# Attention with soft-capped scores and a routed mixture of experts: heads dealt anew to the column strips of sums and gates, and their rounds moved by a step

## Chip, cores and metric

The kernel runs on 1 core of one Trainium2 chip. The metric is device time in microseconds (us), measured on the chip. TensorE is called PE here, VectorE DVE, ScalarE ACT, GpSimd POOL, and SP is the engine that issues most transfers.

## What is computed

```python
# batch 8, heads 12, sequence 448, head size 64; cap = 30; 8 experts
scores = (q @ k.T) / 8
scores = cap*tanh(scores/cap);  scores -= max
attn = exp(scores);  attn /= attn.sum(-1) + 1e-9
x = (attn @ v) as [3584 tokens, 768]
logits = x @ w_gate                    # [3584, 8]
# tokens are taken in the order of their best logit, each expert takes 448
out[tokens of e] = relu(x[tokens of e] @ w1[e]) @ w2[e]
```

All is in fp32. The routing needs every logit of every batch before the first expert's tokens are known, so the attention stage ends before the experts start.

## The kernel before

**Steps.** `attention` takes a batch in three steps of four heads (m=0, 1, 2); step g of 24 runs from L253. In a step PE computes seven score tiles (`qk`, L149 and L154) into pS, a PSUM pool of two buffers; ACT empties each with a tanh (L155) and follows with three exps over groups (L159). Attention times values of the step before (`avq`, L187) runs between the scores into pT, two banks. DVE transposes the next step's q and k (`tr`, L135), adds the exps over the key blocks (`esum`, L163: 'e1' late in the own step, 'e2' and 'r' in the next) and copies the finished values out as xT (`av_out`, L197).

**Sums and gates.** The softmax denominators and the products with w_gate are computed together by short matmuls of 32 output columns, dealt to four column strips of the array (`rnd`, L204): four matmuls, one on each strip, are a *round*. An 's' item multiplies by ones and sums es of one head; a 'g' item multiplies xT of a pair of heads by gates (gw). A plan deals the 12 heads to the strips. Batches 0 to 6 deal them by `h//3`: every round holds heads of all three steps, five rounds a batch, two issued in the second step of the next batch and three in its third. The last batch is dealt by `h%4`: six rounds, two for each step's heads, so that the first four can be issued before the last heads are done.

**Logits and turns.** `logit_in` (L208) copies the strips' result to lg, `logit` transposes it on PE (L215), and DVE takes the reciprocal of the sums (L221, kept as rin), scales, and reduces over the heads to the logits (L228, L231, L237). `xt` (L37, L45) turns one pair of heads of xT back to token order on PE and multiplies by rin on DVE into xn, which is written to DRAM as xs. For batches 0 to 3 this is done inside the stage, six pairs a batch, four of them in the first step of the batch after the next and two in its second. For batches 4 to 7 it is deferred to the routing, where ACT and POOL do it.

**What sets the order.** PE, ACT, DVE and SP run their instructions in the order of the code; POOL is scheduled for it. All of rounds, logits' transposes and the stage's `xt` draw their PSUM tiles from pM, which has two banks, given out in turn: a third tile needs the first one's last reader to be done. After the last step comes a tail: the remaining values, the last rounds, and the logits of batch 7 in two pieces. Behind it the routing starts (L462 and on), a chain of short operations.

Of the kernel before, what the change touches and what calls it, by code (L numbers as in the profile page):

```python
# [17 lines left out]
def attention(nc, tc, c1, xp, pM, q, k, v, cap, w_gate, xs, L1, ident, on_logits, on_turn, NDEF, xd, setup):  # L18
# [7 lines left out]
    def xt(b,p,late=None):  # L26
# [11 lines left out]
        def rest():  # L38
            src=ps[:CP,:].rearrange("p (j h d) -> p j h d",j=NJ,h=2)
            if late:  # L40
# [5 lines left out]
                rin[b][:,:,2*p:2*p+2].unsqueeze(3).broadcast_to([CP,NJ,2,D]),op=ALU.mult)  # L46
# [5 lines left out]
    with ExitStack() as ctx:  # L52
# [53 lines left out]
        locA,blkA=plan(lambda h:h//3)  # L106
        locB,blkB=plan(lambda h:h%4)
        gw=c2.tile([128,len(blkA)+len(blkB),32],F32,name="gw")
        nc.gpsimd.memset(gw,0.0)
        wgs=c2.tile([128,NP,E],F32,name="wgs")  # L110
        def gates():
# [3 lines left out]
            for o,loc,blk in ((0,locA,blkA),(len(blkA),locB,blkB)):  # L115
                for bi,(g,p,hs) in enumerate(blk):
                    if len(hs)==2:
                        assert loc[hs[1]][1]==loc[hs[0]][1]+1
                    for h in hs:
                        l=loc[h][1]; hp=slice(h%2*64,h%2*64+64)  # L120
                        nc.gpsimd.tensor_copy(gw[hp,o+bi,3+8*l:11+8*l],wgs[hp,h//2,:])
        rA=[[] for _ in range(5)]
        for g in range(4):
            seq=[('s',l,3*g+l) for l in range(3)]+[('g',bi,p) for bi,(gg,p,hs) in enumerate(blkA) if gg==g]
            for r in range(5): rA[r].append((g,)+seq[r])
        rB={}
        for m in range(3):
            rB[m]=[[(locB[h][0],'s',locB[h][1],h) for h in range(4*m,4*m+4)],
                   [(g,'g',len(blkA)+bi,p) for bi,(g,p,hs) in enumerate(blkB) if 4*m<=hs[0]<4*m+4]]

# [57 lines left out]
        def av(g,o,j):  # L188
            if j==0: avp[g,o]=pT.tile([128,512],F32,name="psA")
            z=nats[g,2][0]  # L190
            for h in range(2):
                nc.tensor.matmul(avp[g,o][h*64:h*64+64,:S],z[:,j,HG*h+o,:],ev(g,2*j+o)[:,h,:],start=(j==0),stop=(o==1 and j==2))
# [16 lines left out]
        def logit(b,l0,l1,part=None,final=True):  # L209
# [3 lines left out]
            ps=pM.tile([128,512],F32,name="psM")  # L213
# [5 lines left out]
            rv=r.rearrange("p j (g l) -> p j g l",l=3) if b<B-1 else r.rearrange("p j (l g) -> p j g l",l=3)  # L219
# [33 lines left out]
        for g in range(N):  # L253
# [6 lines left out]
            if 0<=bb-1<B-NDEF and m<2:  # L260
                for p in ((0,1),(4,5))[m]: xt(bb-1,p)
            if m==2 and bb>=0:
                for r in (2,3,4): rnd(bb,rA[r],False,r==4)
            for j in range(3): avq(g-1,j,0)
            tr(g+1,0)
            if m==2 and bb>=0:
# [6 lines left out]
            if m==0:  # L273
                if 0<=bb-1<B-NDEF: xt(bb-1,2); xt(bb-1,3)
# [642 lines left out]
```

## Time and profile before

| | |
|---|---|
| median of 3 runs | 922.61 us (920.12 to 923.22) |
| the profiled execution | 919.02 us |
| its span | 916.9 us |
| attention stage, first to last round of the tail | about the first 340 us |
| PE, DVE, ACT, POOL busy in the span | 96%, 63%, 62%, 38% |

A row of a timeline has the start and busy time in us, the engine, the line and operation, the tile written and those read, the shape, how many instructions stand in the row, and in brackets how long the engine was idle before it and what ended that. Busy times of rows overlap a little, since the ends of pipelined instructions are modelled: what a group takes is read from its start to the next one's. An fp32 matmul shows as two instructions.

### The profile page before, as it was taken

How to read it: one execution, taken by the hardware profiler on the slowest of the kernel's cores; microseconds unless marked ns; L12 is line 12 of the kernel's file. 1: busy time of each engine (PE TensorE's matmuls, PEld its weight loads, DVE VectorE, ACT ScalarE, POOL GpSimd, SP SyncE). 2: the span in 40 equal slices, each digit the busy share in tenths (PEclk: the TensorE clock that was granted, in tenths of full speed). 3: DMA queues.
4: the chain of work that ended last, by engine and by line, in shares of the span. 5: the costliest groups of instructions: out<-in, count | busy, mean ns of one | idle time of the engine just before them, and what ended most of it. 6: DMA issues, size and time to landing. Idle time of an engine off the chain costs nothing.

```text
span 916.9 us, 17474 instructions
## 1 busy us (share of the span) xinstructions
PE 879.8 (96%) x6338; PEld 639.3 (70%) x6338; DVE 578.6 (63%) x1932; ACT 570.7 (62%) x796; POOL 346.1 (38%) x474
## 2 busy tenths in 40 slices
PE   7899999999999996799999999999999999999996
PEld 3333444444333345689989989889989889999996
DVE  3778988989778688766756656556666564231210
ACT  6999999999999947273462561662652642522520
POOL 5200000000000008482593592592682763754831
PEclk9999999999999999799999999999999999999999
DMA  8899999987992017741813616406407407326201
GB/s 123 113 136 129 139 165 173 135 161 135 189 151 74 1 38 250 241 171 50 307 40 126 237 35 230 150 18 233 155 10 250 147 3 267 127 82 239 76 9 52
DMA packets 291702, 123.07 MB, mean 134 GB/s; under 512 B 224768, under 2 KB 275712, under 8 KB 291104
## 3 DMA queue, kind: packets, MB, share of 16 engines
q1 hardware_dynamic: 285104, 99.70, 47.8%
q0 software_dynamic: 4656, 22.02, 6.4%
q8 instruction: 50, 0.82, 0.4%
q10 hardware_dynamic: 1856, 0.23, 0.2%
q14 instruction: 36, 0.29, 0.1%
HBM read 97.15 MB, written 24.77 MB: 133 GB/s over the span
## 4 chain that ended last, share of the span: by engine, by line
PE 73%; issue 9%; ACT 9%; POOL 3%; DVE 3%; DMA 1%; SPq 0%; POOLq 0%; ACTq 0%; DVEq 0%
PE psH L768 23%; PE psH L796 21%; PE psA L187 10%; PE psS L149 8%; ACT e L155 5%; PE psM L204 3%; ACT e L159 3%; PE psS L154 2%; PE psX L739 2%; POOL out_dram L781 1%; POOL w1l L700 1%; DMA xg<-xs,idx 1%; PE psL L37 1%; DVE cmpD L462 1%; POOL w2l L700 1%
## 5 line engine op out<-in xcount | busy, mean ns | idle before, releaser
L796 PE MATMUL psH<-w2h,hh 128*128 128x384 f32 x896 | 249.7, 344 | 0.0
L796 PE MATMUL psH<-w2l,hh 128*128 128x384 f32 x512 | 174.3, 340 | 0.0
L155 ACT ACTIVATE e<-psS,s 128x896 f32<-128x896 f32 x168 | 160.5, 994 | 16.5 <-PE psS L149 8.8
L796 PEld LDWEIGHTS psH<-w2h,hh 128*128 128x128 f32 x896 | 162.8, 189 | 0.2
L159 ACT ACTIVATE e<-e,bias,capt 128x1792 f32<-128x1792 f32 (+2 forms) x74 | 154.2, 2084 | 2.5
L768 PE MATMUL psH<-xgh,w1h 128*128 128x448 f32 x384 | 143.0, 372 | 0.3 <-ACT xgh L744 0.3
L768 PE MATMUL psH<-xgl,w1h 128*128 128x448 f32 x384 | 141.8, 370 | 0.0
L768 PE MATMUL psH<-xgh,w1l 128*128 128x448 f32 x384 | 141.7, 369 | 0.0
L149 PE MATMUL psS<-tq,tk 64*64 64x448 f32 x1152 | 130.7, 548 | 11.3 <-ACT e L155 11.2
L45 POOL TENSOR_TENSOR xn<-raw,rin 112x512 f32<-112x512 f32 x24 | 24.4, 1049 | 307.7 <-ACT raw L42 306.7
L700 POOL TENSOR_TENSOR w2l<-w2r,w2h 128x768 fp32r<-128x768 f32 x64 | 118.0, 1843 | 12.2 <-ACT w2h L696 12.2
L700 POOL TENSOR_TENSOR w1l<-w1r,w1h 128x768 fp32r<-128x768 f32 x62 | 114.1, 1841 | 21.6 <-ACT w1h L696 17.4
L187 PE MATMUL psA<-e,nv 64*64 64x448 f32 x1104 | 120.5, 543 | 0.5 <-DVE xT L197 0.5
L163 DVE TENSOR_TENSOR es<-es,e 64x896 f32<-64x896 f32 (+2 forms) x74 | 100.5, 1359 | 4.9 <-ACT e L159 3.5
L802 ACT ACTIVATE on<-psH 128x384 f32<-128x384 f32 x48 | 23.6, 491 | 126.4 <-PE psH L796 123.8
L776 DVE SCALAR_TENSOR_TENSOR hh<-psH,hh 128x64 fp32r<-128x64 f32 (+1 forms) x128 | 44.1, 386 | 90.6 <-ACT hh L774 90.3
L149 PEld LDWEIGHTS psS<-tq,tk 64*64 64x64 f32 x1152 | 42.2, 133 | 78.8 <-ACT e L155 43.4
L796 PEld LDWEIGHTS psH<-w2l,hh 128*128 128x128 f32 x512 | 96.5, 189 | 0.0
L187 PEld LDWEIGHTS psA<-e,nv 64*64 64x64 f32 x1104 | 44.9, 134 | 61.9 <-issue 50.4
L768 PEld LDWEIGHTS psH<-xgh,w1h 128*128 128x128 f32 x384 | 72.6, 189 | 5.6 <-ACT xgh L744 0.5
L768 PEld LDWEIGHTS psH<-xgh,w1l 128*128 128x128 f32 x384 | 72.4, 189 | 5.2
L768 PEld LDWEIGHTS psH<-xgl,w1h 128*128 128x128 f32 x384 | 72.5, 189 | 5.0
(263 smaller groups left out, 1216.4 us busy)
## 6 DMA issues: line engine op xcount, KB each, us to landing
w1r<-in_moe_w_dram SPq DMA_DIRECT2D x64, 384.0 KB, 3.9
w2r<-in_moe_w_dram SPq DMA_DIRECT2D x32, 768.0 KB, 7.7
k<-in_k_dram SPq DMA_DIRECT2D x92, 112.0 KB, 3.4
q<-in_q_dram SPq DMA_DIRECT2D x92, 112.0 KB, 3.9
nv<-in_v_dram SPq DMA_DIRECT2D x72, 128.0 KB, 3.8
xs<-xn SPq DMA_DIRECT2D x4, 1344.0 KB, 7.3
xs<-xn SPq DMA_DIRECT2D x4, 896.0 KB, 5.1
xd<-xT SPq DMA_DIRECT2D x2, 1344.0 KB, 7.1
```

What stands on the lines that cost most here:

```text
L45: (nc.gpsimd if late else nc.vector).tensor_tensor(xn[b][:,:,h0:h0+3:2,:],src, rin[b][:,:,2*p:2*p+2].unsqueeze(3).broadcast_to([CP,NJ,2,D] ...
L149: for c in range(2): nc.tensor.matmul(ps[c*64:c*64+64,h,:S],tks[g,0][hp,o,u*128+c*64:u*128+c*64+64],tks[g,1][hp,o,:],start=True,stop=True)
L155: nc.scalar.activation(ev(g,r),ps[:,:,:S],AF.Tanh,scale=s1)
L159: nc.scalar.activation(e,e,AF.Exp,scale=capt,bias=bias)
L163: t=es_t[g]; add=lambda o,a,b: nc.vector.tensor_tensor(o,a,b,op=ALU.add)
L187: nc.tensor.matmul(avp[g,o][h*64:h*64+64,:S],lhs,rhs[hp,h,:],start=(j==0 and x==0),stop=(j==3 and (g<N-1 or o==0)))
L204: nc.tensor.matmul(ps[g*32:g*32+32,:S],lhs,rhs,start=first,stop=last)
L700: (eng or nc.gpsimd).tensor_tensor(view(l),r,view(h).bitcast(F32),op=ALU.subtract)
L768: nc.tensor.matmul(ps[:,:C],a[:,c,:],b[:,c,:],start=(m==0),stop=(m==DC*3-1)); m+=1
L776: nc.vector.scalar_tensor_tensor(h[:,d:d+b-a],ps[:,a:b],0.0,h[:,a:b].bitcast(F32),op0=ALU.max,op1=ALU.subtract)
L796: nc.tensor.matmul(ps[:,:HD],h[:,f,a:a+128],spl[p,2,hf,f//2][w][:,f%2,:],start=(m==0),stop=(m==nm-1))
L802: if t<3: nc.scalar.activation(ons[p][0][:,t*DM+hf*HD:t*DM+hf*HD+HD],ps[:,:HD],AF.Copy)
```

## The change

One plan takes the place of two: `h//2 if h<8 else h-8`. Heads 0 to 7 fill the strips two by two, heads 8 to 11 follow one by one, so the first three rounds (two of sums, one of gates for four pairs) need only the first two steps' heads, and the last two only the third step's. All batches have five rounds, and gw shrinks from 20 blocks to 8. Since a pair's two heads no longer lie side by side in rin for the last two pairs, `xt` reads those with a stride of 3.

In the steps, what belongs to the batch before moves:

| | before | now |
|---|---|---|
| rounds 1, 2 | second step, after the fourth score tile | first step, after the fourth score tile |
| rounds 3 to 5 and the copy to lg | third step, ahead of the values | second step, ahead of the values |
| logits | third step, after the fourth score tile | third step, ahead of the values |
| `xt`, pairs 0 to 2 (batches 0 to 3) | first step of the next batch | third step, after the fourth score tile |
| `xt`, pairs 3 and 4 | first and second step | first step, ahead of the values |
| `xt`, pair 5 | second step | second step, ahead of the values |

At the end, the last step's first value matmuls (`av`) move into the last step and take a pM bank, and the tail has five rounds in another order.

```diff
             (nc.gpsimd if late else nc.vector).tensor_tensor(xn[b][:,:,h0:h0+3:2,:],src,
-                rin[b][:,:,2*p:2*p+2].unsqueeze(3).broadcast_to([CP,NJ,2,D]),op=ALU.mult)
+                rin[b][:,:,slice(3*p,3*p+2) if p<4 else slice(6*p-22,6*p-18,3)].unsqueeze(3).broadcast_to([CP,NJ,2,D]),op=ALU.mult)
...
-        locA,blkA=plan(lambda h:h//3)
-        locB,blkB=plan(lambda h:h%4)
+        loc,blk=plan(lambda h:h//2 if h<8 else h-8)
...
+        s_=lambda l: [(loc[h][0],'s',l,h) for h in range(H) if loc[h][1]==l]
+        g_=lambda n: [(g,'g',bi,p) for bi,(g,p,hs) in enumerate(blk) if len(hs)==n]
+        R=[s_(0),s_(1),g_(2),s_(2),g_(1)]
...
             qk(g,0); qk(g,1)
             if 0<=bb-1<B-NDEF and m<2:
-                for p in ((0,1),(4,5))[m]: xt(bb-1,p)
-            if m==2 and bb>=0:
-                for r in (2,3,4): rnd(bb,rA[r],False,r==4)
+                for p in ((3,4),(5,))[m]: xt(bb-1,p)
+            if m==1 and bb>=0:
+                for r in (2,3,4): rnd(bb,R[r],False,r==4)
+            if m==2 and bb>=0: logit(bb,0,3)
             for j in range(3): avq(g-1,j,0)
             tr(g+1,0)
-            if m==2 and bb>=0:
+            if m==1 and bb>=0:
                 logit_in(bb)
...
             for w in ('e2','r'): esum(g-1,w)
             qk(g,2); qk(g,3)
             if m==0:
-                if 0<=bb-1<B-NDEF: xt(bb-1,2); xt(bb-1,3)
+                if bb>=0: rnd(bb,R[0],True,False); rnd(bb,R[1],False,False)
                 if bb>0: on_logits(bb-1)
-            if m==1 and bb>=0: rnd(bb,rA[0],True,False); rnd(bb,rA[1],False,False)
-            if m==2 and bb>=0: logit(bb,0,3)
             if m==1 and bb>0: on_turn(bb-1)
+            if m==2 and 0<=bb<B-NDEF:
+                for p in range(3): xt(bb,p)
+            if last: av(g,0,0)
             tr(g+1,1)
...
-            if last:
-                rnd(b,rB[0][0],True,False); rnd(b,rB[0][1],False,False)
-                av(g,0,0); av(g,0,1)
         g=N-1; b=B-1
-        rnd(b,rB[1][0],False,False); rnd(b,rB[1][1],False,True)
+        av(g,0,1)
+        rnd(b,R[0],True,False); rnd(b,R[1],False,False)
         esum(g,'o1')
-        av(g,0,2); av(g,1,0)
+        av(g,0,2)
+        rnd(b,R[2],False,True)
         esum(g,'o2')
         logit_in(b)
+        av(g,1,0); av(g,1,1)
         esum(g,'r')
-        part=logit(b,0,2,final=False)
-        av(g,1,1)
         avq(g,3,1)
         av_out(g,0)
+        part=logit(b,0,2,final=False,pool=pT)
         av(g,1,2)
         av_out(g,1)
-        rnd(b,rB[2][0],True,False)
-        rnd(b,rB[2][1],False,True)
+        rnd(b,R[3],True,False)
+        rnd(b,R[4],False,True)
         logit(b,2,3,part=part)
```

How the instructions stand is shown at three places. The changed kernel's lines up to `rnd` lie ten lower: L139 is the old L149, L177 the old L187, L182 the old L192, L194 the old L204, L205 the old L215, and on DVE L125, L153, L187, L211, L218, L221, L227 are the old L135, L163, L197, L221, L228, L231, L237.

First, PE in the third step of batch 2. Before, from the gate rounds (L204) to the fifth score tile (L149):

```order
L204 MATMUL psM_1238<-xT_871,gw_135 32x448 x8
L187 MATMUL psA_1335<-e0_1178,nv_1008 64x448 x2
L187 MATMUL psA_1336<-e0_1178,nv_1008 64x448 x2
L187 MATMUL psA_1335<-e1_1224,nv_1008 64x448 x2
L187 MATMUL psA_1336<-e1_1224,nv_1008 64x448 x2
L187 MATMUL psA_1335<-e2_1249,nv_1008 64x448 x2
L187 MATMUL psA_1336<-e2_1249,nv_1008 64x448 x2
L149 MATMUL psS_1357<-tq_1247,tk_1219 64x448 x4
L149 MATMUL psS_1363<-tq_1247,tk_1219 64x448 x4
L215 MATMUL psM_1370<-ident_62,lg_1351 112x128 x4
L149 MATMUL psS_1385<-tq_1247,tk_1219 64x448 x4
```

and now, from the logits' transposes (L205) to the third pair's transposes (L37):

```order
L205 MATMUL psM_1325<-ident_62,lg_1230 112x128 x4
L177 MATMUL psA_1337<-e0_1181,nv_1015 64x448 x2
L177 MATMUL psA_1338<-e0_1181,nv_1015 64x448 x2
L177 MATMUL psA_1337<-e1_1235,nv_1015 64x448 x2
L177 MATMUL psA_1338<-e1_1235,nv_1015 64x448 x2
L177 MATMUL psA_1337<-e2_1251,nv_1015 64x448 x2
L177 MATMUL psA_1338<-e2_1251,nv_1015 64x448 x2
L139 MATMUL psS_1357<-tq_1249,tk_1228 64x448 x4
L139 MATMUL psS_1363<-tq_1249,tk_1228 64x448 x4
L37 MATMUL psM_1371<-ident_62,xT_873 112x128 x4
L37 MATMUL psM_1377<-ident_62,xT_873 112x128 x4
L37 MATMUL psM_1383<-ident_62,xT_873 112x128 x4
```

The rounds are gone from the step, the logits stand where they stood, and where the logits stood are three pairs' transposes: three tiles of pM in a row (psM_1371, 1377, 1383), and a fourth (psM_1325) a little ahead.

Second, DVE in the same step. Before, from the transpose of k (L135) to the late addition (L163):

```order
L135 STREAM_TRANSPOSE tk_1349<-k_1017 128x896
L208 COPY lg_1351<-psM_1238 128x448
L163 TENSOR_TENSOR es_1285<-es_1285,e2_1249 128x1792
L163 TENSOR_TENSOR es_1285<-es_1285,e2_1249 64x896 x2
L221 RECIPROCAL rg3_1376<-psM_1370 112x48
L228 TENSOR_TENSOR lt3_1378<-psM_1370,rg3_1376 112x384
L231 TENSOR_REDUCE L1_67<-lt3_1378 112x32
L237 COPY rin_1375<-rg3_1376 112x48
L135 STREAM_TRANSPOSE tq_1382<-q_1022 128x896
L163 TENSOR_TENSOR es_1420<-e0_1309,e1_1356 128x1792
```

and now, from the reciprocal (L211) to the transpose of q (L125):

```order
L211 RECIPROCAL rg3_1331<-psM_1325 112x48
L218 TENSOR_TENSOR lt3_1333<-psM_1325,rg3_1331 112x384
L221 TENSOR_REDUCE L1_67<-lt3_1333 112x32
L227 COPY rin_1330<-rg3_1331 112x48
L125 STREAM_TRANSPOSE tk_1351<-k_1024 128x896
L153 TENSOR_TENSOR es_1287<-es_1287,e2_1251 128x1792
L153 TENSOR_TENSOR es_1287<-es_1287,e2_1251 64x896 x2
L45 TENSOR_TENSOR xn_1370<-psM_1371,rin_1330 112x4x2x64
L45 TENSOR_TENSOR xn_1370<-psM_1377,rin_1330 112x4x2x64
L45 TENSOR_TENSOR xn_1370<-psM_1383,rin_1330 112x4x2x64
L125 STREAM_TRANSPOSE tq_1389<-q_1029 128x896
```

The logit block moved ahead of the transpose and of the additions to es, the copy to lg went to the step before, and the multiplies that read the three tiles stand behind the additions.

Third, PE in the tail. Before, from the second pair of values (L192) on:

```order
L192 MATMUL psA<-e_3324,nv 64x448 x2
L204 MATMUL psM<-es,ones 32x448 x4
L204 MATMUL psM<-xT,gw 32x448 x4
L192 MATMUL psA<-e_3368,nv 64x448 x2
L192 MATMUL psA<-e_3279,nv 64x448 x2
L215 MATMUL psM<-ident,lg 112x128 x4
L192 MATMUL psA<-e_3324,nv 64x448 x2
L187 MATMUL psA<-e_3368,nvh 64x448 x4
L192 MATMUL psA<-e_3368,nv 64x448 x2
L204 MATMUL psM<-es,ones 32x448 x4
L204 MATMUL psM<-xT,gw 32x448 x4
```

and now, from the second pair of values (L182) on:

```order
L182 MATMUL psM<-e_3342,nv 64x448 x2
L194 MATMUL psM<-es,ones 32x448 x8
L182 MATMUL psM<-e_3359,nv 64x448 x2
L194 MATMUL psM<-xT,gw 32x448 x4
L182 MATMUL psA<-e_3281,nv 64x448 x2
L182 MATMUL psA<-e_3342,nv 64x448 x2
L177 MATMUL psA<-e_3359,nvh 64x448 x2
L177 MATMUL psM<-e_3359,nvh 64x448 x2
L205 MATMUL psA<-ident,lg 112x128 x4
L182 MATMUL psA<-e_3359,nv 64x448 x2
L194 MATMUL psM<-es,ones 32x448 x4
L194 MATMUL psM<-xT,gw 32x448 x4
```

The first three rounds are gathered between values of the last step, the old order's two rounds ahead of these rows are gone, and the logits' transposes follow one value pair and the remainder's values.

29 lines of the change are left out of this document (9 added, 20 removed).

## Prediction

> **What bounds the kernel now.** I read the page first: TensorE (PE) is busy in 96% of the span, but its tenths sink only around slices 14 to 16, between the attention stage and the experts. The change touches only the attention stage and its last few microseconds, so I then asked for the busy time in stretches cut where a step of that stage begins (the first score matmul on PE). Eight batches have three steps each. I call the steps of a batch first, second and third (m=0, 1, 2). The columns are the stretch, its length, busy time and count of PE, weight loads, VectorE (DVE), ScalarE (ACT) and POOL, the granted clock, DMA share and GB/s.
>
> ```profile
> 45.12:85.21 40.09, 38.27 (x385) 14.55 (x380) 32.00 (x30) 38.43 (x31) 0.00 (x0) 1.00 1.03 135
> 85.21:207.39 122.18, 121.62 (x1217) 52.11 (x1213) 107.33 (x159) 115.65 (x91) 0.00 (x0) 1.00 0.96 153
> 166.68:179.83 13.15, 12.96 (x133) 5.59 (x125) 11.89 (x30) 12.79 (x11) 0.00 (x0) 1.00 0.99 138
> 179.83:193.57 13.74, 13.74 (x141) 6.62 (x141) 12.16 (x11) 12.87 (x11) 0.00 (x0) 1.00 0.82 182
> 193.57:207.39 13.82, 13.82 (x145) 5.16 (x141) 11.71 (x13) 12.89 (x11) 0.00 (x0) 1.00 0.97 135
> 207.39:248.25 40.86, 40.67 (x410) 17.47 (x406) 35.94 (x54) 38.55 (x31) 0.00 (x0) 1.00 0.83 162
> 248.25:288.34 40.09, 38.08 (x385) 13.64 (x381) 32.54 (x47) 38.44 (x31) 0.00 (x0) 1.00 0.83 143
> 288.34:314.60 26.26, 24.25 (x244) 8.47 (x240) 20.82 (x34) 25.54 (x21) 0.00 (x0) 1.00 0.01 2
> 314.60:340.16 25.56, 25.56 (x229) 8.33 (x222) 20.18 (x42) 16.68 (x14) 0.00 (x0) 1.00 0.01 1
> ```
>
> Rows one, two, six and seven are batches 1, 2 to 4, 5 and 6. The last two are batch 7: its two first steps, then its third step with the tail. Rows three to five are the steps of batch 4. Where PE has transposes and rounds to do besides scores and values, it is busy all the time (13.74 of 13.74, 13.82 of 13.82). Where it has little (26.26 for two steps), ACT sets the pace: 13.13 a step. So PE and ACT lie within 0.7 us of each other, DVE a little behind (107.33 of 122.18), and a new wait on PE is paid nearly in full.
>
> Next, PE's rows of two steps, in order of time (start, busy, engine, line, tiles, count, idle before).
>
> ```profile
> 174.50 0.98 PE L149 MATMUL psS<-tq,tk 64*64 64x448 f32 x8 [0.19 <-ACT e L155]
> ...
> 179.83 1.74 PE L149 MATMUL psS<-tq,tk 64*64 64x448 f32 x16
> 181.49 1.09 PE L37 MATMUL psM<-ident,xT 128*112 128x128 f32 x8
> 182.51 2.67 PE L187 MATMUL psA<-e,nv 64*64 64x448 f32 x24
> ...
> 193.57 1.68 PE L149 MATMUL psS<-tq,tk 64*64 64x448 f32 x16
> 195.18 0.96 PE L204 MATMUL psM<-es,ones 128*32 128x448 f32 x8
> 195.96 1.69 PE L204 MATMUL psM<-xT,gw 128*32 128x448 f32 x16
> 197.57 2.49 PE L187 MATMUL psA<-e,nv 64*64 64x448 f32 x24
> 199.88 1.68 PE L149 MATMUL psS<-tq,tk 64*64 64x448 f32 x16
> 201.49 0.65 PE L215 MATMUL psM<-ident,lg 128*112 128x128 f32 x4
> 202.07 0.98 PE L149 MATMUL psS<-tq,tk 64*64 64x448 f32 x8
> ```
>
> From start to start these give the parts of a step: two scores 1.61, two transposes 1.02 (one 0.51), three rounds 2.39, three values 2.31, the logits' transposes 0.58. From the fifth score tile (174.50) to the next step (179.83) it is always 5.33. ACT stands against it so:
>
> ```profile
> 173.47 1.89 ACT L155 ACTIVATE e<-psS,s 128x896 f32<-128x896 f32 x2
> ...
> 198.56 1.88 ACT L159 ACTIVATE e<-e,bias,capt 128x1792 f32<-128x1792 f32 x1
> 200.88 1.91 ACT L155 ACTIVATE e<-psS,s 128x896 f32<-128x896 f32 x2 [0.43 <-PE psS L149]
> ```
>
> The fifth score tile needs the buffer that the third tanh empties: that tanh began at 173.47, the matmul at 174.50, 1.03 later. In a third step the third tanh could start at 6.87 after the step's start (198.56 and 1.88, less 193.57) but waited for PE until 7.31. So the fifth score starts at the later of PE's own list and third tanh + 1.03, and a step is that plus 5.33.
>
> **The change part by part.** *Rounds and logits, one step earlier.* The new first step has two transposes and two rounds: the very list of the old second step, 13.74 (row four). Without transposes (batches 1, 6, 7) it stays at ACT's 13.13. The new second step has one transpose and three rounds ahead of the values: the third tanh waits for PE until 7.31 + 0.51 = 7.82, the fifth score starts at 8.85, the step takes 14.18 (13.74 if PE never waited; I take 14.18, as the wait of 0.43 is in the trace). Without the transpose it is 7.31 + 1.03 + 5.33 = 13.67.
>
> *Three transposes in the third step.* PE comes to them at 1.61 + 0.58 + 2.31 + 1.61 = 6.11 and is through two at 7.13. The third has no bank: pM has two, so it needs the one whose reader is the first multiply (L45) on DVE, and by the new order that multiply stands behind the es additions. DVE's prices:
>
> ```profile
> 198.25 4.23 DVE L163 TENSOR_TENSOR es<-es,e 128x1792 f32<-128x1792 f32 x3
> 202.41 0.44 DVE L221 RECIPROCAL rg<-psM 112x48 f32<-112x48 f32 x1
> ...
> 204.36 1.09 DVE L135 STREAM_TRANSPOSE tq<-q 128x896 f32<-128x896 f32 x1
> ```
>
> and for the multiplies, two in a row:
>
> ```profile
> 209.69 1.29 DVE L45 TENSOR_TENSOR xn<-psM,rin 112x512 f32<-112x512 f32 x2 [0.82 <-PE psM L37]
> ```
>
> The logits' matrices leave PE at about 1.61 + 0.65 = 2.26. Then DVE runs the logit block 1.95 (202.41 to 204.36), a transpose of k 1.09, three additions 4.16 (198.25 to 202.41) and one multiply 0.65 (half of 1.29): 10.11, with some 0.04 for the handover to PE, an estimate, 10.15. PE stood ready at 7.13 and waits 3.0. The fifth score starts at 10.15 + 0.51 = 10.66 and the step takes 16.0. ACT catches nothing up: tanh and exp behind the fifth score keep their distance to the next step. Bounds of the wait: 2.4 if the first addition overlaps what stands ahead of it, 3.4 if the handovers and the refilling of PE cost what the model of ends hides; I keep 3.0. It is met once in each of batches 1 to 4, the only ones transposed inside the stage, and replaces a step of 13.82. Batches 5 to 7 have no transposes there and fall to ACT's 13.13.
>
> *The tail.* Six rounds become five, and one value matmul pair moves into the last step, where ACT is waited for.
>
> ```profile
> 330.17 1.72 PE L192 MATMUL psA<-e,nv 128*64 128x448 f32 x8
> ```
>
> On DVE the logit block and the xT copies behind it:
>
> ```profile
> 336.39 0.34 DVE L221 RECIPROCAL rg<-psM 112x32 f32<-112x32 f32 x1
> ...
> 337.84 1.32 DVE L197 COPY xT<-psA 128x448 f32<-128x448 f32 x2
> ```
>
> A pair is 0.86 (half of 1.72), a round 0.80 (a third of 2.39). The last step loses the rounds ahead of its values and falls from a PE list of 13.82, as in row five, to ACT's 6.87 + 1.03 + 5.33 = 13.23: 0.6. At most the three give 2.3. Against it stands DVE: the last round needs the second xT copy, which now comes behind the logit block of 1.45 (336.39 to 337.84) and two copies; counted through, that holds the last round back by about 0.8. I take 1.55, with 0 and 2.3 as the ends.
>
> *At nothing:* half the gate copies on POOL (idle until late in the stage), the strided rin view (the multiplies keep their shape), the spill to xd one step earlier (nobody reads it back before the tail).
>
> **Sum**, against the profiled execution. Batch 1: 13.13 + 13.67 + 16.0 = 42.80 for 40.09, +2.71. Batches 2 to 4: 3 × (13.74 + 14.18 + 16.0) = 131.76 for 122.18, +9.58. Batch 5: 13.74 + 14.18 + 13.13 = 41.05 for 40.86, +0.19. Batch 6: 39.93 for 40.09, −0.16. Batch 7: 26.80 for 26.26, +0.54, and −1.55 in last step and tail. Together +11.3. What follows the tail is a chain of short steps through DVE, PE and DMA and moves as a whole. The profiled execution took 919.02 (span 916.9) and would take 930.3. It lies 3.6 under the median of the runs, 922.61, so for a median I say 933.9.
>
> **The rivals.** *The clock drops in the new wait* (slower still). The trace has a drop where PE is nearly idle, and none in waits of 1.82:
>
> ```profile
> 256.07 0.98 PE L149 MATMUL psS<-tq,tk 64*64 64x448 f32 x8 [1.82 <-ACT e L155]
> ```
>
> Filler matmuls at full clock, then after the drop, and the clock's stretch (0.55 in the third column from the end):
>
> ```profile
> 360.79 1.14 PE L655 MATMUL psX<-ident 128*128 128x128 f32 x8
> ...
> 376.03 5.17 PE L655 MATMUL psX<-ident 128*128 128x128 f32 x24
> ```
>
> ```profile
> 370.00:375.00 5.00, 3.03 (x14) 2.32 (x13) 3.57 (x17) 0.00 (x0) 0.62 (x1) 0.55 0.85 256
> ```
>
> At half clock 24 filler matmuls took 5.17 where 3 × 1.14 = 3.42 would do: 1.75 lost per recovery. Four waits of 3.0 at that price give 4 × 1.75 = 7.0 more, 940.9. For it: 3.0 is longer than any wait of this stage so far. Against it: PE is dense on both sides, and the drop came in a stretch in which PE does little for long (3.03 of 5.00, its fillers at half speed counted in). I give it 0.09. The Trainium skill, page "TensorE: Matmul & The Clock Gate", Part 1, says that the clock falls to half after an idle window of about 3.4 us and comes back after a busy one. By that rule a wait of 3.0 just stays under it, and with 0.4 more it would pay. The trace agrees with it so far, with a clock of 1.00 in every row of this stage and 0.55 behind the long idle.
>
> *The third transpose finds its bank free* (not slower). The place is the third step of batches 1 to 4: if DVE did the first multiply before PE arrives at 7.13, the wait would be gone and the step 13.13. The sum is then −0.16 + 3 × (41.05 − 40.73) + 0.19 − 0.16 + 0.54 − 1.55 = −0.2, 922.4. It decides from a multiply that ends under 7.1 instead of 10.1; for that the additions, 4.16 of it, would have to come after it, and the order has them before. Its chain also cannot start before the logits leave PE at 2.26. I give it 0.06.
>
> *No new wait, and the second step without its ACT wait and the tail at its best*: −0.2 − 4 × 0.44 − 0.75 = −2.7, 919.9, on the edge of what counts as faster: 0.03.
>
> **How the numbers follow.** Forecast 0.82, clock 0.09, free bank 0.06, all gains 0.03. A difference of 0.3%, 2.8 us, is about what a measurement of this kernel tells from none; faster 0.03, within it 0.06, slower 0.91. The forecast's own ends: waits of 2.4 to 3.4 (−2.4, +1.6), the second step's 0.44 in four batches (−1.8, 0), the tail (−0.75, +1.55), not all at once, and some 1.5 for the median: 928.5 to 938.5. The other cases, 0.18, are left out.
>
> **What would show it.** In the profile after: in the third step of batches 1 to 4 a wait of about 3.0 on PE ahead of the third transpose, released by DVE's L45; those steps at about 16.0; DVE without idle time between logits and multiply; second steps at 14.2 with PE waiting 0.4 for ACT; the tail 1.5 shorter; the granted clock at 1.00. The forecast is wrong if the wait is under 1, if later steps give it back, or if the clock falls in the stage.

## The result and the profile after

The changed kernel takes 938.07 us (median of 6 runs, 937.44 to 938.96), the kernel before 922.61: ratio 1.0171, 95% interval 1.0158 to 1.0185. The point forecast was 933.9 and the range 928.5 to 938.5: the time is inside by 0.4, and 4.2 above the point. The profiled execution took 938.96 (span 937.2) against 919.02 (916.9).

The stretches of the stage in the changed kernel, cut where its steps begin (stretch, length, busy time of PE, weight loads, DVE, ACT and POOL, granted clock, DMA share, GB/s). Rows one and two are batch 1 and batches 2 to 4; then the first and second step of batch 4; the third steps of batches 1 to 4; batches 5 and 6; batch 7's first two steps; its third step with the tail.

```profile
47.14:91.69 44.55, 41.05 (x396) 15.32 (x392) 32.40 (x32) 38.66 (x31) 0.00 (x0) 0.96 1.01 138
91.69:227.49 135.80, 125.86 (x1216) 49.88 (x1212) 108.42 (x159) 116.31 (x91) 0.00 (x0) 0.96 0.78 135
180.70:194.20 13.50, 13.50 (x140) 5.34 (x136) 12.24 (x28) 12.88 (x11) 0.00 (x0) 1.00 0.50 81
194.20:208.47 14.27, 13.89 (x145) 5.12 (x141) 10.85 (x11) 12.89 (x11) 0.00 (x0) 1.00 0.80 178
...
73.97:91.69 17.72, 14.78 (x132) 6.17 (x128) 13.03 (x15) 12.99 (x11) 0.00 (x0) 0.90 1.00 140
119.46:136.92 17.46, 14.52 (x133) 6.19 (x128) 13.03 (x15) 13.01 (x11) 0.00 (x0) 0.90 0.93 136
164.68:180.70 16.02, 13.09 (x133) 5.73 (x128) 13.03 (x15) 12.99 (x11) 0.00 (x0) 1.00 0.86 118
208.47:227.49 19.02, 16.08 (x132) 6.59 (x128) 13.04 (x15) 12.99 (x11) 0.00 (x0) 0.82 0.81 125
...
227.49:268.38 40.89, 39.03 (x397) 14.97 (x393) 34.53 (x51) 38.54 (x31) 0.00 (x0) 1.00 0.70 142
268.38:308.34 39.96, 37.76 (x385) 13.60 (x380) 32.61 (x47) 38.44 (x31) 0.00 (x0) 1.00 0.85 146
308.34:335.16 26.82, 26.26 (x269) 9.16 (x265) 21.34 (x35) 25.66 (x21) 0.00 (x0) 1.00 0.01 2
335.16:359.26 24.10, 23.36 (x196) 7.28 (x188) 19.68 (x41) 16.57 (x14) 0.00 (x0) 1.00 0.00 1
```

Read the column of the clock first. In the rows of the stage before (from 45.12 on) it is 1.00 everywhere; here it is 0.90, 0.90, 1.00 and 0.82 in the four third steps that have the new transposes. The one without a loss, batch 3, takes 16.02, the forecast's 16.0. The others, of batches 1, 2 and 4, take 1.70, 1.44 and 3.00 more: 6.14 together.

The wait itself is in PE's rows of two of these steps, batch 3 and batch 4 (start, busy, line, tiles, count, idle before).

```profile
174.81 0.65 PE L37 MATMUL psM<-ident,xT 128*112 128x128 f32 x4 [2.93 <-DVE xn L45]
...
176.19 1.68 PE L177 MATMUL psA<-e,nv 64*64 64x448 f32 x16
...
218.61 1.10 PE L37 MATMUL psM<-ident,xT 128*112 128x128 f32 x4 [2.94 <-DVE xn L45]
...
221.19 3.21 PE L177 MATMUL psA<-e,nv 64*64 64x448 f32 x16
```

The waits are equal; what follows is not. The same four transposes take 0.65 and 1.10, the same values 1.68 and 3.21: half speed. And DVE in batch 4, from the logit block to the last multiply, shows why PE waited:

```profile
210.77 0.46 DVE L211 RECIPROCAL rg<-psM 112x48 f32<-112x48 f32 x1 [0.82 <-PE psM L205]
211.26 0.56 DVE L218 TENSOR_TENSOR lt<-psM,rg 112x384 f32<-112x384 f32 x1
211.85 0.86 DVE L221 TENSOR_REDUCE L<-lt 112x32 f32<-112x384 f32 x1
212.62 0.19 DVE L227 COPY rin<-rg 112x48 f32<-112x48 f32 x1
212.71 1.12 DVE L125 STREAM_TRANSPOSE tk<-k 128x896 f32<-128x896 f32 x1
213.74 4.21 DVE L153 TENSOR_TENSOR es<-es,e 128x1792 f32<-128x1792 f32 x3
217.88 1.27 DVE L45 TENSOR_TENSOR xn<-psM,rin 112x512 f32<-112x512 f32 x2
```

From the logit block to the multiplies DVE has no idle time. The first multiply starts at 217.88 and takes about half of the 1.27 of the two; PE's third transpose starts at 218.61, when it is done.

**Where the 20.3 us of span went.** From the first step of batch 1 to the end of the tail: 359.26 − 47.14 = 312.12, before 295.04 (45.12 to 340.16), so 17.1 more. The forecast's sum was +11.3 for this stage, and 11.3 + 6.14 for the clock is 17.4. Ahead of batch 1 another 2.0 came, 1.7 of it from a clock drop behind a wait of 1.82 on ACT that ended at 40.14: the third step of batch 0 takes 14.83 for 13.14. The kernel before has the same wait there, without a drop. Behind the tail 1.2 came.

### The profile page after: what moved, and what is told of

Same layout as the page of the kernel before. It is cut to its first block, busy times and chain, and to the rows that moved or that the text cites. A ratio compares the mean times of both kernels' runs of the same rounds, so it can differ in the third digit from the quotient of the medians.

```text
span 937.2 us, 17440 instructions
## 1 busy us (share of the span) xinstructions
PE 886.3 (95%) x6330; PEld 635.8 (68%) x6330; DVE 580.2 (62%) x1932; ACT 571.7 (61%) x796; POOL 344.5 (37%) x462
## 4 chain that ended last, share of the span: by engine, by line
PE 73%; issue 9%; ACT 7%; DVE 5%; POOL 3%; DMA 2%; POOLq 0%; SPq 0%; DVEq 0%; ACTq 0%
PE psH L759 23%; PE psH L787 21%; PE psA L177 10%; PE psS L139 8%; ACT e L145 4%; PE psM L194 3%; ACT e L149 2%; PE psS L144 2%; PE psX L730 2%; DVE es L153 1%; DMA xg<-xs,idx 1%; PE psM L37 1%; POOL out_dram L772 1%; DVE cmpD L453 1%; POOL w1l L691 1%
## 5 line engine op out<-in xcount | busy, mean ns | idle before, releaser
L149 ACT ACTIVATE e<-e,bias,capt 128x1792 f32<-128x1792 f32 (+2 forms) x74 | 154.2, 2084 | 2.5
L45 POOL TENSOR_TENSOR xn<-raw,rin 112x512 f32<-112x512 f32 x24 | 24.4, 1054 | 328.1 <-ACT raw L42 327.1
L139 PE MATMUL psS<-tq,tk 64*64 64x448 f32 x1152 | 131.7, 554 | 11.9 <-ACT e L145 11.9
L177 PE MATMUL psA<-e,nv 64*64 64x448 f32 x1104 | 123.1, 556 | 0.2 <-ACT e L149 0.2
L153 DVE TENSOR_TENSOR es<-es,e 64x896 f32<-64x896 f32 (+2 forms) x74 | 100.4, 1358 | 3.5 <-ACT e L149 2.1
L139 PEld LDWEIGHTS psS<-tq,tk 64*64 64x64 f32 x1152 | 40.9, 134 | 85.2 <-ACT e L145 49.0
L177 PEld LDWEIGHTS psA<-e,nv 64*64 64x64 f32 x1104 | 42.4, 137 | 66.2 <-issue 57.5
```

Source lines behind the costliest of these rows:

```text
L45: (nc.gpsimd if late else nc.vector).tensor_tensor(xn[b][:,:,h0:h0+3:2,:],src, rin[b][:,:,slice(3*p,3*p+2) if p<4 else slice(6*p-22,6*p-18 ...
L139: for c in range(2): nc.tensor.matmul(ps[c*64:c*64+64,h,:S],tks[g,0][hp,o,u*128+c*64:u*128+c*64+64],tks[g,1][hp,o,:],start=True,stop=True)
L149: nc.scalar.activation(e,e,AF.Exp,scale=capt,bias=bias)
L153: t=es_t[g]; add=lambda o,a,b: nc.vector.tensor_tensor(o,a,b,op=ALU.add)
L177: nc.tensor.matmul(avp[g,o][h*64:h*64+64,:S],lhs,rhs[hp,h,:],start=(j==0 and x==0),stop=(j==3 and (g<N-1 or o==0)))
```

## The experiments

In the first expectations theory A is the forecast's bank wait together with its rival on the clock: the third transpose waits for the bank that the first multiply frees, and each such wait can also cost clock. B and C put the loss elsewhere, as each expectation says. Later ones give the letters anew. The first times are counted from 922.61 for the kernel before. The ratios are to that kernel measured beside each run, where it took 921.45 or 921.47.

**The additions behind the multiplies.** In third steps with transposes:

```
-            for w in ('e2','r'): esum(g-1,w)
+            esum(g-1,'e2')
+            if not (m==2 and 0<=bb<B-NDEF): esum(g-1,'r')
 ...
                 for p in range(3): xt(bb,p)
+                esum(g-1,'r')
```

> The changed kernel, but in the third steps of batches 1 to 4 the two short additions to es ('r') stand behind the three multiplies on DVE instead of ahead of them. Same work, same banks. Theory A (PE waits for the bank that DVE's first multiply frees, and each such wait can also cost clock): the multiply comes 2.1 us earlier, the wait of 2.94 falls to about 0.8, the granted clock stays at 1.00 behind it, the steps go to 13.9; time 938.07 - 4 x 2.1 - (4 to 6 of clock) = 924 to 926. Theory B (the wait costs only its own length, what the clock lost comes from elsewhere): 938.07 - 8.4 = 929.7. Theory C (the loss is PE's new list, not this wait): no change, 938.

Measured: 923.03 (10 runs), ratio 1.0012, interval 0.9998 to 1.0025. PE's row in batch 1, and the third step of batch 1:

```profile
81.19 0.65 PE L37 MATMUL psM<-ident,xT 128*112 128x128 f32 x4 [0.71 <-DVE xn L45]
```

```profile
73.28:87.08 13.80, 13.09 (x132) 5.73 (x128) 12.41 (x15) 12.88 (x11) 0.00 (x0) 1.00 0.97 130
```

Two short additions moved on DVE take the wait from 2.94 to 0.71, the clock back to 1.00, and nearly all of the loss away. With 1.1 off for the faster kernel beside it, theory A's 924 to 926 fits; B's 929.7 and C's 938 are out. The cause sits in this place. It doesn't tell bank wait from clock, as both went.

**Only two pairs in the third step,** so that no transpose needs a bank that is still being read; the others stand in the first two steps.

```
-                for p in ((3,4),(5,))[m]: xt(bb-1,p)
+                for p in ((2,3),(5,))[m]: xt(bb-1,p)
 ...
             if m==0:
+                if 0<=bb-1<B-NDEF: xt(bb-1,4)
 ...
-                for p in range(3): xt(bb,p)
+                for p in range(2): xt(bb,p)
```

> The changed kernel, but only two pairs are turned back in the third step; the third goes with the fourth into the first step ahead of the values, the fifth into the first step ahead of the rounds. No tile of the third step then needs a bank that is still to be read. Theory A: no wait of PE on DVE's multiplies there, clock 1.00, steps of about 14.25, 14.2 and 13.13 us, 41.6 a batch; time 922.6 + 1.9 = 924.5. Theory B (clock lost elsewhere): some 4 more, 928.7. Theory C (moving rounds and logits a step earlier is what costs): 933 to 938.

Measured: 922.41 (10 runs), ratio 1.0015, interval 1.0002 to 1.0027: a little under theory A's 924.5, far from B and C. The first two steps of batch 2 take 14.08 and 14.27; its third:

```profile
115.32:128.46 13.14, 12.52 (x129) 5.27 (x125) 11.88 (x14) 12.78 (x11) 0.00 (x0) 1.00 1.00 197
```

Without the third transpose the step falls to ACT's 13.14. The bank is the reason for the wait, not DVE's load as such: DVE still does the additions there, ahead of two multiplies.

**Filler matmuls in the wait,** to keep PE busy and leave the bank wait: first 14, then 8, into the score buffer that the next score matmul overwrites anyway.

```
-                for p in range(3): xt(bb,p)
+                xt(bb,0); xt(bb,1)
+                fill=pS.tile([128,2,512],F32,name="psS")
+                for _ in range(8): nc.tensor.matmul(fill[:,0,:128],ident,ident,start=True,stop=True)
+                xt(bb,2)
```

> The changed kernel with 14 filler matmuls of 128 columns, about 2.0 us, ahead of the third transpose in the third steps of batches 1 to 4, written to the score buffer that the next score tile overwrites. The bank is freed no earlier, so the transposes start where they did; only PE's idle time falls from 2.9 to two pieces of at most 0.9. Theory A: clock 1.00 through these steps, steps of 16.0 each, time 933.9 (932.5 to 934.5), which is what the sum without a clock drop gave. Theory B (the clock loss has nothing to do with idle time there): 938. If the fillers delay the transposes: above 938.

Measured with 14: 935.28 (4 runs), ratio 1.0149 (1.0119 to 1.0180). That is above the expected 932.5 to 934.5. The size was misjudged: the 14 fillers, 28 instructions, ran 3.39 instead of 2.0 and held the third transpose back by about 0.9, so part of the clock's gain was spent again (clock 1.00, third steps 16.9). With 8:

> The changed kernel with 8 filler matmuls instead of the 14 of the filler run before, which ran 3.2 us and held the third transposes back by 0.9. Eight last 1.85 us: from 7.8 after the step's start to 9.7, before the bank is free at 10.1. Theory A (bank wait plus clock): the third transposes start at 10.1 to 10.2 after the step's start as without fillers, PE idles 0.6 and then 0.4, the clock stays at 1.00 in all four places, the steps take 16.0; time 935.3 - 4 x 0.9 = 931.7, about 6 less than the changed kernel. Theory B (fillers change nothing but the delay they caused): 938 - 0 = 938. If idle time of under 1 us in two pieces still costs clock: 933 to 936.

Measured: 930.38 (4 runs), ratio 1.0094 (1.0073 to 1.0116). PE in batch 4, and the third steps of batches 1 and 4 (16.04 in the other two, with the same clock):

```profile
213.18 2.05 PE L271 MATMUL psS<-ident 128*128 128x128 f32 x16 [0.62 <-ACT e L145]
215.50 0.65 PE L37 MATMUL psM<-ident,xT 128*112 128x128 f32 x4 [0.27 <-DVE xn L45]
```

```profile
73.96:89.98 16.02, 15.14 (x148) 7.59 (x144) 13.03 (x15) 13.00 (x11) 0.00 (x0) 1.00 0.97 134
205.36:221.39 16.03, 15.14 (x148) 7.59 (x144) 13.04 (x15) 13.00 (x11) 0.00 (x0) 1.00 0.82 119
```

This kernel does more work than the changed one and is faster, near theory A's 931.7. The third transposes still wait for DVE, the four steps take the forecast's 16.0 to 0.04, and the clock is 1.00 in all of them. So the two parts stand side by side: 0.9% (8.7 us of 921.45) without the clock's part, 1.7% with it; the difference of the two ratios, 0.0077, is some 7 us for the clock. From the first step of batch 1 to the end of the tail the profiled execution of this kernel takes 306.06 (47.13 to 353.19), 11.0 more than before: the forecast's +11.3, without the clock's part.

**The tail alone** (the old order in the steps, the new dealing and the new end):

```
-                for p in ((3,4),(5,))[m]: xt(bb-1,p)
-            if m==1 and bb>=0:
+                for p in ((0,1),(4,5))[m]: xt(bb-1,p)
+            if m==2 and bb>=0:
                 for r in (2,3,4): rnd(bb,R[r],False,r==4)
```

and so on, back to the old places, from `if last: av(g,0,0)` on as in the change.

> The kernel before with the new dealing of heads for all batches and the new last step and tail, but the rounds, logits and turns in the steps where they were. Theory A: no wait in the third steps, and the last step and tail are bound by the chain through DVE (copies of xT, additions, copy to lg, logits, second copy of xT); with the rounds of batch 6 still ahead of the values, the last step is 14.7 instead of 13.2 and everything behind it shifts, so from the last step's start to the end of the last round it takes about 25.5, no gain; time 922.6. Rival: PE alone bounds the tail and the round that is gone shows, 24.7, time 921.8. If the tail made by itself what the change gained there, 24.1 and 921.2.

Measured: 921.47 (10 runs), ratio 0.9997 (0.9983 to 1.0011). Its third step of batch 7 with the tail:

```profile
317.10:342.75 25.65, 25.65 (x220) 7.97 (x213) 20.21 (x42) 16.64 (x14) 0.00 (x0) 1.00 0.01 1
```

That is theory A's "about 25.5, no gain": 25.65 against 25.56 before. The 1.46 that the changed kernel gains there (25.56 to 24.10) needs the rounds out of the last step as well: in this stretch the two kernels differ only in these rounds, their copy to lg and the place of the logits.

**One of the two short additions behind the multiplies,** a wait between 0.71 and 2.94:

```
-            for w in ('e2','r'): esum(g-1,w)
+            for w in ('e2','r0') if m==2 and 0<=bb<B-NDEF else ('e2','r'): esum(g-1,w)
 ...
                 for p in range(3): xt(bb,p)
+                esum(g-1,'r1')
```

> The changed kernel with one of the two short additions to es moved behind the multiplies in the third steps of batches 1 to 4, the other left ahead: the wait of 2.94 (0.71 with both moved) should become 1.9. Bank theory: steps of 14.9. Clock: if a wait has to be longer than about 2 to cost clock, none here, 938.07 - 4 x 1.05 - 6.4 = 927.5 or a little below; if 1.9 costs as 2.94 did, 933.9; if in some of the four places, between. Rival (no clock loss by waits): 933.9 too, but with a clock of 1.00 at the four places.

Measured: 932.95 (4 runs), ratio 1.0123 (1.0097 to 1.0149). The third step of batch 1, and PE's row in it:

```profile
72.81:89.54 16.73, 14.77 (x132) 6.11 (x128) 13.03 (x15) 12.98 (x11) 0.00 (x0) 0.90 0.93 133
```

```profile
81.97 0.65 PE L37 MATMUL psM<-ident,xT 128*112 128x128 f32 x4 [1.96 <-DVE xn L45]
```

The wait is 1.96 in all four places, and the clock falls in all four: third steps of 16.7, where 16.0 less 0.98 of wait gives 15.0. So the branch "1.9 costs as 2.94 did" (933.9) came, and the rival with a clock of 1.00 is out. But a wait of under 2 us lost 1.7 of clock each time, and one of 2.93 in batch 3 of the changed kernel lost none: the length of the wait alone does not decide. What does?

**The clock's grid.** Read in stretches of 0.2 us, the clock changes in this stage of the changed kernel at 40.47 (down), 43.88 (up), 84.84, 88.26, 129.22, 132.63, 217.96, 224.79. Every distance is a whole number of 3.413 us: 84.84 − 40.47 = 13 × 3.413, 129.22 − 84.84 = 13, 217.96 − 129.22 = 26, 224.79 − 217.96 = 2. Cut on this grid, the four waits in the changed kernel look so (two stretches each for batches 1, 2 and 3, three for batch 4):

```profile
81.43:84.84 3.41, 0.73 (x8) 0.56 (x12) 3.25 (x5) 3.08 (x3) 0.00 (x0) 1.00 0.48 106
84.84:88.26 3.42, 3.42 (x20) 1.10 (x20) 3.42 (x3) 1.01 (x1) 0.00 (x0) 0.50 1.10 164
125.80:129.22 3.42, 0.86 (x8) 0.62 (x6) 3.37 (x4) 3.39 (x4) 0.00 (x0) 1.00 0.92 136
129.22:132.63 3.41, 3.03 (x16) 1.48 (x20) 2.81 (x5) 0.99 (x2) 0.00 (x0) 0.50 0.90 139
170.18:173.59 3.41, 1.70 (x16) 0.84 (x8) 3.36 (x3) 3.38 (x4) 0.00 (x0) 1.00 0.61 100
173.59:177.00 3.41, 2.19 (x24) 1.13 (x28) 3.27 (x5) 2.23 (x2) 0.00 (x0) 1.00 0.47 68
...
214.55:217.96 3.41, 1.12 (x12) 0.84 (x8) 3.36 (x4) 3.38 (x4) 0.00 (x0) 1.00 0.37 65
217.96:221.38 3.42, 2.77 (x16) 1.43 (x20) 2.82 (x4) 1.09 (x1) 0.00 (x0) 0.50 0.63 91
221.38:224.79 3.41, 3.41 (x24) 1.02 (x20) 1.99 (x2) 1.01 (x1) 0.00 (x0) 0.50 0.74 116
```

Second and third number are length and PE's busy time. Where PE was busy for 0.73, 0.86 and 1.12 of a stretch (idle 2.68, 2.56, 2.29), the next one runs at half clock. In batch 3 a line of the grid cuts the wait into idle times of 1.71 and 1.22, and the clock stays. In batch 4 the end of the wait, 0.65, lies in the slow stretch, and a second slow one follows; that is its 3.00 instead of 1.7. The rule read from this: the idle sum of one stretch of the grid decides, somewhere between 1.5 and 1.85 us. It was put to the test in further runs.

The changed kernel and the one with waits of 1.96, unchanged, again:

> The changed kernel once more, unchanged, to test a rule read from the traces so far: the granted clock changes only at instants a whole number of 3.41 us apart, and it is halved for the stretch that follows if PE was idle for 1.85 us or more of the stretch of 3.41 that ended there, whatever the length of the single wait. By the rule (theory A): all changes of the clock in this trace lie whole multiples of 3.413 apart; of the four waits of 2.9, those drop the clock that leave 1.85 or more of idle time in one such stretch, and one that the grid cuts into two parts of 1.5 or less does not; between 1.5 and 1.85 either may come. The grid's place against the program is not the same in each execution, so three waits in four is not a fixed count. Rival B, the length of a wait decides alone: all four drop, or the same three as before (batches 1, 2 and 4). Rival C, chance without a grid: changes of the clock at distances that are no multiples of 3.413.

> The kernel with one of the short additions behind the multiplies (waits of 1.96), once more, unchanged. By the rule of stretches of 3.41 us (theory A): a wait of 1.96 drops the clock where it lies inside one stretch, or with 1.85 of it; where the grid cuts it so that no stretch holds more than 1.5, the clock stays at 1.00 and the third step takes about 15.0 instead of 16.7. A wait without a drop makes the batch 42.8 instead of 44.5, which is 12.5 stretches instead of 13.0, so the next wait stands half a stretch further in the grid and should drop. Rival B, the length of the wait decides alone: four drops of four, as in the first look, wherever the grid stands. Rival C: no grid.

> The same kernel a third time, so that the grid stands elsewhere. The same expectations: by theory A each wait drops if 1.85 or more of it lies in one stretch of 3.41, and does not if no stretch holds more than 1.5 of idle time; by B all four drop; by C no grid.

Measured: 938.01, 933.72 and 933.77 (one run each, before 923.38). Every change of the clock lies on a grid of 3.413 again. The drops in these waits are the same three and the same four, each behind a stretch with 1.95 or more of idle time; so the grid is borne out, but the rule is not told apart from "the same waits drop each time", as all fell into similar places: inconclusive on that. One thing more speaks for the grid: in the last of the three its lines stand about 0.8 later, and the drop comes at 83.34 with the wait over at 82.00, while in the first execution of the same kernel it came at 82.57 with the wait over at 81.97. The drop follows the grid, not the wait.

So the waits were moved against the grid, with extra filler work in the first steps of batches 2 to 4, where PE has no gap: four fillers a batch, then six.

```
+            fill=None
+            if m==0 and 1<=bb<B-NDEF:
+                fill=pS.tile([128,2,512],F32,name="psS")
+                for _ in range(4): nc.tensor.matmul(fill[:,0,:128],ident,ident,start=True,stop=True)
-            qk(g,2); qk(g,3)
+            qk(g,2,fill); qk(g,3)
```

> One short addition behind the multiplies (waits of 1.96 in four third steps), and four filler matmuls of about 0.23 each on PE in the first steps of batches 2 to 4, where PE is busy without a gap: they shift each later wait against the clock's grid of 3.413 us by some 0.9 more than before. The waits themselves stay as long as they were. Theory A (grid; the idle share of a stretch of 3.41 decides): a wait with 1.85 or more in one stretch drops the clock at that stretch's end, third step 16.7; a wait cut so that neither stretch holds over 1.5 does not, third step 15.0. At least one of the four should now be cut so, and which ones can be read from the trace by where the other changes of the clock put the grid. Rival B (the length of the wait alone): four drops, four third steps of 16.7.

> The same with six fillers, some 1.4 per batch, so that the waits behind the first one stand elsewhere again. With the grid standing as in the first look at the kernel without fillers, where the waits began 0.85 after a grid line, the first wait drops the clock, and the next begins about 2.3 after one and is cut into parts of about 1.1 and 0.9: by theory A no drop there and 15.0 for that third step; a batch without a drop is 44.2, 12.9 stretches, so the third and fourth would begin at about 2.15 and 1.95 and be cut too, the last into 1.46 and 0.5. With the grid elsewhere the pattern differs, and the rule (1.85 or more in one stretch drops, 1.5 or less does not) decides each. Rival B: four drops of four.

Measured: 934.12 and 930.59 (one run each, before 921.83). The waits are 1.95 to 1.97 in all eight places. With four fillers the stretches that hold the waits of batches 1 to 4 (the first row of each pair) read:

```profile
79.39:82.81 3.42, 1.46 (x15) 1.04 (x17) 3.21 (x5) 3.39 (x4) 0.00 (x0) 1.00 1.39 147
82.81:86.22 3.41, 3.41 (x20) 1.15 (x21) 3.41 (x4) 1.71 (x2) 0.00 (x0) 0.50 0.99 133
123.77:127.18 3.41, 2.13 (x20) 1.08 (x16) 3.35 (x4) 3.41 (x3) 0.00 (x0) 1.00 1.37 149
127.18:130.60 3.42, 2.74 (x28) 1.38 (x32) 3.27 (x5) 3.07 (x3) 0.00 (x0) 1.00 1.24 164
168.14:171.56 3.42, 1.83 (x20) 0.88 (x12) 3.35 (x3) 3.39 (x4) 0.00 (x0) 1.00 0.65 108
171.56:174.97 3.41, 3.04 (x32) 1.53 (x36) 3.26 (x5) 2.81 (x2) 0.00 (x0) 1.00 0.64 92
212.51:215.93 3.42, 1.53 (x16) 0.84 (x8) 3.35 (x4) 3.39 (x4) 0.00 (x0) 1.00 0.19 37
215.93:219.34 3.41, 3.35 (x19) 1.51 (x23) 2.81 (x5) 1.96 (x2) 0.00 (x0) 0.50 0.89 135
```

Two of four dropped: idle 1.96 and 1.89 did, 1.28 and 1.59 did not. With six fillers no wait costs clock:

```profile
80.01:83.42 3.41, 2.19 (x24) 1.13 (x28) 3.23 (x5) 3.16 (x3) 0.00 (x0) 1.00 1.35 171
124.38:127.80 3.42, 2.06 (x20) 1.07 (x24) 3.24 (x5) 3.19 (x3) 0.00 (x0) 1.00 1.19 154
168.75:172.17 3.42, 1.92 (x20) 1.07 (x24) 3.24 (x5) 3.18 (x4) 0.00 (x0) 1.00 0.72 113
213.13:216.54 3.41, 1.76 (x18) 0.92 (x21) 3.23 (x5) 3.17 (x4) 0.00 (x0) 1.00 0.63 103
```

The expected pattern of this kernel (first wait drops, the others not) missed in its first place: the grid stood elsewhere against the program, and the first wait was cut too. The fillers also took longer than expected, 1.25 and 1.70 a first step (14.75 and 15.20 for 13.50) for 0.9 and 1.4. With six a batch takes 44.5, about 13 stretches, so its four waits test nearly one place in the grid, not four. No place speaks against the rule (1.59 and 1.65 lie in its open zone), and "the length of the wait alone" is out: equal waits of 1.96 dropped the clock twice and left it six times.

**The dealing and the tail kept, the steps of batches 2 to 5 as before.** In batches 1, 6 and 7, which have no transposes in their first two steps, the rounds stand early; in the tail the second value output goes ahead of the logit block.

```
+            own=0<=bb-1<B-NDEF
+            if own and m<2:
+                for p in ((0,1),(4,5))[m]: xt(bb-1,p)
+            if bb>=0 and own and m==2:
+                for r in (2,3,4): rnd(bb,R[r],False,r==4)
+            if bb>=0 and not own and m==1: rnd(bb,R[2],False,False)
+            if bb>=0 and not own and m==2: logit(bb,0,3)
 ...
+            if bb>=0 and m==(1 if own else 0): rnd(bb,R[0],True,False); rnd(bb,R[1],False,False)
 ...
+            if bb>=0 and not own and m==1:
+                for r in (3,4): rnd(bb,R[r],False,r==4)
 ...
-        part=logit(b,0,2,final=False,pool=pT)
         av(g,1,2)
         av_out(g,1)
+        part=logit(b,0,2,final=False,pool=pT)
```

> The changed kernel's dealing and tail, with the steps chosen by batch: where transposes of an earlier batch stand in the stage (the steps of batches 2 to 5) rounds, logits and turns are placed as before the change; in the others (batches 1, 6, 7) rounds 1 and 2 go to the first step, round 3 ahead of the values of the second and rounds 4 and 5 behind its fourth score tile, logits ahead of the values of the third. In the tail the second xT copy goes ahead of the logit block on DVE. Theory: steps without transposes all fall to ACT's 13.13 (39.4 instead of 40.1 a batch in batches 1 and 6, nothing in 7's first two), the last step and tail take 23.3 instead of 25.5; together -0.7 - 0.7 - 2.2 = -3.6, 0.996 of the kernel before, no wait on DVE's multiplies. Rival (rounds ahead of the fifth score delay tanh and exp by more than PE gains): 1.000 or more.

Measured: 917.29 (6 runs, 916.71 to 918.86), ratio 0.9957 (0.9940 to 0.9974): 0.4% faster than the kernel before, as expected. Its batches 1 and 6 take 39.65 (before 40.09; 39.4 was expected, but the second steps take 13.38, not 13.13), and its last step with the tail 23.28 (before 25.56). So the early rounds gain in steps without transposes. The tail gains 0.82 more than in the changed kernel, with the second xT copy ahead of the logit block.

## Why the prediction was right, and where it was not

- *The case and the time.* The number lies inside the range, but the case that came is the rival with 0.09. By the prediction's own words the forecast is wrong "if the clock falls in the stage", and it fell. From profiled execution to profiled execution the sum gave 930.3, and 938.96 came. That the median stays inside is in part luck: the range reaches 938.5 by margins for the wait, the tail and the median, while wait and tail came as forecast; the loss of clock filled the room left for them.
- *The bank wait.* Forecast 3.0 in the third step of batches 1 to 4, released by L45. Measured 2.94 (2.93 once), four times, and 16.02 for the step where the clock stayed. Right, and the two edits that move additions or take the third transpose away show the cause.
- *First and second steps.* Forecast 13.74 and 14.18; measured 13.50 and 14.27. Batches 5, 6 and 7's first two steps: forecast 41.05, 39.93 and 26.80; measured 40.89, 39.96 and 26.82. Right to 0.25.
- *Tail.* Forecast −1.55, measured −1.46. Right in its parts too, as far as they were tried: the 0.8 for the second xT copy behind the logit block is the 0.82 that came back when the copy went ahead. But with the rounds left in the last step the new tail gave nothing, where a round and a pair less 0.8 would give 0.9: the gains do not simply add.
- *At nothing.* The prediction calls POOL idle until late in the stage. It is busy for 17.86 of the first 45.12 us, ahead of the rows that the prediction shows; nothing in the time was traced to it.
- *The clock.* "The granted clock at 1.00" failed. The rival that it drops in the new wait had 0.09, and it happened in three waits of four: 6.14 us in the profiled execution where that rival said 7.0. Its price of 1.75 per recovery was right (1.70 measured for one slow stretch of 3.41 at half speed), its chance was not. Both arguments against it failed. "PE is dense on both sides" does not protect, since a stretch of 3.41 is judged by itself. And "none in waits of 1.82" is a misreading of the trace of before. That kernel waits 1.82 on ACT five times, and behind one of these waits, in batch 0, the clock falls:

```profile
17.30 0.98 PE L154 MATMUL psS<-tq,tk 64*64 64x448 f32 x8 [1.82 <-ACT e L155]
18.34 2.84 PE L149 MATMUL psS<-tq,tk 64*64 64x448 f32 x16
```

```profile
15.54:18.95 3.41, 1.59 (x16) 0.44 (x16) 1.87 (x2) 3.21 (x4) 0.00 (x0) 1.00 0.88 122
18.95:22.36 3.41, 3.41 (x20) 1.21 (x20) 1.31 (x2) 3.38 (x3) 0.00 (x0) 0.50 0.75 120
```

The two scores take 2.84 where two others take 1.68. The drop lies ahead of 45.12, where the prediction's rows begin. It also cost nothing there: the second step of batch 0 takes 13.64, and 13.78 without a drop in the changed kernel, as PE still had idle time in that step. The wait of 1.82 that the prediction shows, ended at 256.07, was not safe by its length: a line of the grid cuts it (the clock of before changes at 18.95, 22.36, 370.52 and 380.76, whole numbers of 3.413 apart):

```profile
251.05:254.47 3.42, 3.20 (x30) 0.62 (x24) 2.98 (x2) 3.39 (x4) 0.00 (x0) 1.00 1.44 176
254.47:257.88 3.41, 1.81 (x20) 0.82 (x24) 3.33 (x21) 3.38 (x4) 0.00 (x0) 1.00 0.47 77
```

- From 22.36 on, the most that one stretch of that kernel was idle in this stage is this 1.60. The Trainium skill, page "TensorE: Matmul & The Clock Gate", Part 1, was used in the prediction for an idle window of about 3.4 us, under which 3.0 just stays. The Trainium skill says there as well that the window is free-running, and in this the traces agree (3.413). They differ on what a window needs for a drop: 1.82 of idle time in one did it in the kernel before, 1.89 with four fillers, and the measurement decides. So "the trace agrees with it so far" held only for the rows shown.
- *What the forecast should have been.* An estimate from the rule: with a drop from 1.85 on, a wait of 2.94 escapes only where the grid cuts it into two parts below that, (2 × 1.85 − 2.94) / 3.41 = 22% of the places; with a drop from 1.5 on, 2%. Three drops in four at 1.7 or a little more is +5 to +6, 939 to 940. The measured median, 938.07, is a little under it, as the bank wait's price in medians is 8.7 where the sum said 11.3 and profiled executions show 11.0: the profiled execution of before was 3.6 under its median. A likely part of that, not shown for the kernel before itself, is that its waits of 1.82 cost clock in some executions and not in others. The kernel with the tail alone, which keeps the old steps, had a drop in the wait that before has at 296.16, and its step took 14.83 for 13.13.

Open: the exact point between 1.5 and 1.85 (stretches with 1.52 and 1.74 of idle time dropped, others with 1.82 did not; ends of matmuls are modelled, so idle times are not exact to that), and what brings the clock back (in this stage 3.03 busy of a slow stretch did and 2.77 did not, but behind it, with 8 and 14 fillers and one addition moved, slow stretches of 2.83, 3.06 and 3.11 did not either).

## What to carry to other kernels

A step that gives PE work whose buffer is freed by another engine is to be priced by that engine's queue in program order: here two short additions ahead of a multiply were nearly the whole cost. A wait on PE can have a second price on top of its length: where it leaves PE idle for about half of a 3.4 us stretch or more, and PE sets the pace behind it, 1.7 us more go, so a wait of about 2 us is to be counted nearly double. Small waits in one stretch add up: in the kernel with two pairs, waits of 0.99 and 0.83 behind the stage left the stretch 347.38 to 350.80 idle for 1.85, and the clock fell at its end. If the wait can't go, a few matmuls into a buffer that is overwritten anyway are cheaper than the clock, as long as they end before the wait does.

## What was not expected of the hardware

- The clock's changes lie on a grid of 3.413 us in all fourteen traces (before, after and twelve experiments), with another offset to the program in different executions.
- From 24 to 358 us every stretch at full clock with 1.85 us or more of idle time on PE was followed by half clock, none with 1.5 or less; between them either came. The wait of 1.82 in the third step of batch 0, which no edit touches, lay whole in one stretch in ten traces: in five the clock fell and the step took 14.83, in five it stayed and the step took 13.13 to 13.20.
- Eight extra matmuls in each wait made the kernel some 7 us faster (ratios 1.0171 and 1.0094). Six in each of three steps without any gap, put there only to shift the waits, left the clock at 1.00 behind all four waits.
- Distances in the program near 13 stretches (44.37) keep their place in the grid: the kernel with waits of 1.96 has batches of 44.5, and all four of its waits dropped the clock in each of three executions.
